# A decode step of gated attention and FFN: the block's barrier moved from behind the stores to behind wo's first piece

## Chip, cores and metric

The kernel runs on one core of a Trainium2 chip. The metric is the device time of one execution in microseconds (us); the times given are medians of several runs. The trace comes from one further execution under the hardware profiler, and its own time is given beside its span, which runs from the program's first to its last instruction.

The engines are named as in the profile: PE (TensorE; PEld are its weight loads), DVE (VectorE), ACT (ScalarE), POOL (GpSimd) and SP (SyncE). A "q" behind an engine's name marks what its sequencer does: it issues DMAs, drains, branches and handles semaphores.

## The reference

One token x (512 values, bf16) goes through two branches, which a gate mixes:

```python
g = sigmoid((x * gate_w).sum())
a = attention(x @ wq, k_cache, v_cache) @ wo      # 32 heads, 8 kv heads, 32768 keys of 128
b = (silu(x @ w_gate) * (x @ w_up)) @ w_down      # 512 -> 1792 -> 512
out = g * a + (1 - g) * b                         # 512 values
```

Each of 8 groups (g) has its own K and V cache of 32768 x 128 values, which 4 query heads share. The two caches are 64 MB each in bf16, the weights some 13 MB; all of it is read once.

## The kernel before

It is written engine by engine, in one block: each engine has a program of its own (`@block.sync`, `@block.tensor`, and so on), and they meet through semaphores alone. At the block's end every engine drains its work, adds to a semaphore, and waits for a release that POOL gives when all have come. This is the block's barrier; a like one stands ahead of the block.

**Loads.** SP issues all loads in one queue, in the order in which they are needed: wq, x and gate_w, w_gate and w_up, then for each group two K and two V blocks of 4 MB each into a ring of pages, each issue waiting until its page is free. Behind the last V block come w_down (`wd`) and wo. wo has 4 MB and is loaded in five pieces, of 8, 10, 8, 4 and 2 of its 32 row blocks (`WO_CUTS`, line 59), each with its own semaphore `sem_wo[k]`. They go into the page that held wq, so they are issued as soon as the V load ahead of them is.

**Attention.** In a loop over groups, PE transposes the K rows as pairs (line 372) and DVE copies them to SBUF (637); PE makes the scores (384); DVE takes maxima (642, 644), POOL reduces them over the partitions (254), ACT takes the exponentials with their sums (540); PE sums the V rows weighted with them into `ps_o` (429), ACT copies that (552), and PE adds up its parts (410).

**The end.** It is part of PE's last trip through the loop, `emit_end` (463). PE sums the exponentials over the partitions (465) and DVE makes the scaled heads `O2` out of them (660 to 676). The output row is summed in two places. `emit_wide` (439) multiplies a 128 x 512 block of wd or wo by one column and adds to `ps_w` (in the profile under `pst`, line 441), in four strips. `emit_rows` (450) multiplies a block in four quarters, each into rows of its own of `ps_c` (line 453). The order is: 8 blocks of wd; the transposition matmul of O2 (479); wo's piece 0 (8 blocks); the other 6 blocks of wd; piece 1 (10 blocks). Then DVE copies `ps_w` to `part` (680), PE adds the four strips of `part` into `ps_c` (the join, line 502), and pieces 2, 3 and 4 follow with `emit_rows`. DVE casts the sum into `res_row` (682), and SP and ACT each store a half of it (`store`, line 203). POOL waits for both stores (257), and then the block's barrier ends the program.

PE's wait for a piece of wo stands in line 487, its waits for the copy and for `O2z` in 500 and 501. `sem_pe_w` and `sem_dve_w` carry the join, `sem_pe_sum` and `sem_dve_row` the end.

Of the kernel before, what the change touches and what calls it, by code (L numbers as in the profile page):

```python
# [13 lines left out]
def bass_gated_mix__gqa_block_cached__swiglu_ffn__decode_kernel(  # L14
# [24 lines left out]
    FC = F // 128  # L39
# [15 lines left out]
    WOJ = H * DH // 128  # L55
# [3 lines left out]
    WO_CUTS = [0, 8, 18, 26, 30, 32]  # L59
    KW = 1  # L60
    WD_CUT = 8
    WIDE = WO_CUTS[KW + 1]
    OC = NOUT // 128

    RQ = 4
    NSTRIP = 4
    RPS = 2
    SW = 32
# [8 lines left out]
    with ExitStack() as es:  # L77
# [6 lines left out]
        sem_wo = [S_(f"s_wo{i}") for i in range(len(WO_CUTS) - 1)]  # L84
# [6 lines left out]
        sem_out = S_("s_out")  # L91
# [10 lines left out]
        sem_pe_sum = S_("s_pe_sum")  # L102
# [11 lines left out]
        sem_dve_oz = S_("s_dve_oz")  # L114
        sem_dve_row = S_("s_dve_row")
        sem_psw = S_("s_psw")
        sem_pe_w = S_("s_pe_w")
        sem_dve_w = S_("s_dve_w")
# [34 lines left out]
        tT = T("tT", [128, FC], BF16)  # L153
        wd = T("wd", [128, FC, NOUT], BF16)
# [9 lines left out]
        sel5 = T("sel5", [128, SW + 15], FP32)  # L164
# [7 lines left out]
        O2 = T("O2", [128, WOJ], BF16)  # L172
        O2z = T("O2z", [128, WOJ - WIDE, SW], BF16)
        part = T("part", [128, NOUT], FP32)
        res_row = T("res_row", [128, 128], BF16)
# [17 lines left out]
        ps_c = pst[1][:, 0:512]  # L193
        ps_w = pst[0][:, 512:1024]
# [5 lines left out]
        wgu = page[:, PG_F, 0 : 2 * KC * F].rearrange("p (w c f) -> p w c f", w=2, c=KC)  # L200
        wo_v = page[:, PG_X, 0 : WOJ * NOUT].rearrange("p (j n) -> p j n", j=WOJ)

        def store(eng, k):
            n = RPS * 128
            eng.dma_start(
                out[0, 0, n * k : n * (k + 1)].rearrange("(c n) -> c n", c=RPS),
                res_row[64 * k + SW - 1 : 64 * k + SW + 1, :],
            ).then_inc(sem_out, 16)

        with nc.Block("main") as block:  # L210
            @block.gpsimd
            def _(pool):
                pool.memset(ones_bf[:, :], 1.0).then_inc(sem_const, 1)
                pool.memset(ones_f[:, :], 1.0).then_inc(sem_const, 1)
                npool = [0]

                def chain(ins):
                    ins.then_inc(sem_pool, 1)
                    npool[0] += 1
                    pool.wait_ge(sem_pool, npool[0])  # L220

                pool.load_library(library_config.all_libraries[1])

                def ones_where(t, base, pattern):
                    return pool.affine_select(
                        out=t,
                        in_=t,
                        compare_op=ALU.not_equal,
                        fill=1.0,
                        base=base,  # L230
                        pattern=pattern,
                        channel_multiplier=1,
                    )

                pool.memset(ident[:, :], 0.0)
                pool.memset(ident_f[:, :], 0.0)
                pool.memset(perm[:, :, :], 0.0)
                pool.memset(sel5[:, :], 0.0)
                chain(pool.memset(pmat[:, :], 0.0))
                ones_where(ident[:, :], 0, [[-1, 128]]).then_inc(sem_ident, 1)  # L240
                ones_where(ident_f[:, :], 0, [[-1, 128]]).then_inc(sem_ident, 1)
                for e in range(2):
                    ones_where(perm[:, e, :], -e, [[0, 2], [-2, 64]]).then_inc(sem_ident, 1)
                ones_where(pmat[:, :], 0, [[-1, 32], [-32, 4]]).then_inc(sem_ident, 1)
                for c in range(NSTRIP):
                    chain(ones_where(sel4, -32 * c, [[-1, 16]]))
                pool.sem_inc(sem_ident, 1)
                pool.wait_ge(sem_dve_gpart, 1)
                pool.partition_all_reduce(gtot[:, :], gpart[:, :], 128, ReduceOp.add).then_inc(
                    sem_gtot, 1  # L250
                )
                for g in range(G):
                    pool.wait_ge(sem_pmax, STEP * (g + 1))
                    pool.partition_all_reduce(  # L254
                        gmax[:, g, :], pmax[:, g * STEP : g * STEP + HPG], 128, ReduceOp.max
                    ).then_inc(sem_gmax, 1)
                pool.wait_ge(sem_out, 32)

            @block.sync
            def _(sp):  # L260
# [47 lines left out]
                sp.wait_ge(sem_pe_q, 1)  # L308
                for k in range(len(sem_wo)):
                    load_wo(k)  # L310
                sp.wait_ge(sem_dve_row, 1)
                store(sp, 0)

            @block.tensor
            def _(pe):
                pe.wait_ge(sem_ld_x, 32)
                pe.wait_ge(sem_const, 1)
                for src, base in ((x_row, M_X0), (gw_row, M_X0 + KC)):
                    srcv = src[0:1, :].rearrange("o (p c) -> o c p", c=KC)
                    for c in range(KC):  # L320
# [4 lines left out]
                            start=True,  # L325
                            stop=True,
# [5 lines left out]
                for h in range(H):  # L332
                    for c in range(KC):
# [4 lines left out]
                            start=(c == 0),  # L338
# [97 lines left out]
                        )  # L436
                    ins.then_inc(sem_v_free, 1)

                def emit_wide(w, vec, j, first, last):
                    c = j % NSTRIP  # L440
                    return pe.matmul(  # L441
                        ps_w[32 * c : 32 * c + 1, :],
                        vec[:, j : j + 1],
                        w[:, j, :],
                        start=first,
                        stop=last,
                        skip_group_check=True,
                    )

                def emit_rows(lhs, rhs, first, last):  # L450
                    for oc in range(OC):
                        e = oc % RPS
                        ins = pe.matmul(  # L453
                            ps_c[32 * oc : 32 * oc + (1 if e else SW), 0:128],
                            lhs(e),
                            rhs[:, oc * 128 : (oc + 1) * 128],
                            start=first,
                            stop=last,
                            skip_group_check=True,
                        )  # L460
                    return ins

                def emit_end():
                    pe.wait_ge(sem_dve_esum2, 1)
                    pe.matmul(  # L465
                        ps_e[:, 0:H],
                        ones_f[:, :],
                        esum2[:, :, :].rearrange("p g h -> p (g h)"),
                        start=True,
                        stop=True,  # L470
                    ).then_inc(sem_pe_S, 1)
                    emit_reduce((G + 1) * STEP)
                    pe.wait_ge(sem_dve_tT, 1)
                    pe.wait_ge(sem_ld_wd, 16)
                    pe.wait_ge(sem_psw, 1)
                    for j in range(WD_CUT):
                        emit_wide(wd, tT, j, j < NSTRIP, False)
                    pe.wait_ge(sem_dve_oT2, 1)
                    pe.matmul(
                        ps_m[:, M_O0 : M_O0 + WOJ], pmat[:, :], O2a[:, :], start=True, stop=True  # L480
                    ).then_inc(sem_pe_O2, 1)
                    pe.wait_ge(sem_dve_O2, 1)
                    for k, s in enumerate(sem_wo):
                        if k == 1:
                            for j in range(WD_CUT, FC):
                                emit_wide(wd, tT, j, False, False)
                        pe.wait_ge(s, 16)
                        for j in range(WO_CUTS[k], WO_CUTS[k + 1]):
                            if j < WIDE:
                                ins = emit_wide(wo_v, O2, j, False, j >= WIDE - NSTRIP)  # L490
                            else:
                                ins = emit_rows(
                                    lambda e: O2[:, j : j + 1] if e else O2z[:, j - WIDE, :],
                                    wo_v[:, j, :],
                                    False,
                                    j == WOJ - 1,
                                )
                        if k == KW:
                            ins.then_inc(sem_pe_w, 1)
                            pe.wait_ge(sem_dve_w, 1)  # L500
                            pe.wait_ge(sem_dve_oz, 1)
                            emit_rows(lambda e: sel5[:, SW - 1 : SW] if e else sel5[:, 0:SW], part, True, False)
                    ins.then_inc(sem_pe_sum, 1)

                with pe.Fori(0, (G + 1) * STEP, STEP) as i:
                    for b in range(NB):
# [13 lines left out]
            def _(act):  # L520
# [37 lines left out]
                    if g:  # L558
                        emit_acc(g - 1)
                emit_acc(G - 1)  # L560
                act.wait_ge(sem_dve_row, 1)
                store(act, 1)

            @block.vector
            def _(dve):
# [110 lines left out]
                dve.tensor_copy(  # L676
                    O2z[:, :, SW - 1], ps_m[:, M_O0 + WIDE : M_O0 + WOJ]
                ).then_inc(sem_dve_oz, 1)
                dve.wait_ge(sem_pe_w, 1)
                dve.tensor_copy(part[:, :], ps_w[:, :]).then_inc(sem_dve_w, 1)  # L680
                dve.wait_ge(sem_pe_sum, 1)
                dve.tensor_copy(res_row[:, :], ps_c[:, 0:128]).then_inc(sem_dve_row, 1)


# [26 lines left out]
```

## Time and profile before

| what | us |
|---|---|
| median of 3 runs | 352.69 (352.42 to 352.89) |
| profiled execution, its own time | 352.48 |
| its span | 350.7 |
| PE busy | 269.5 (77% of the span) |
| DVE busy | 176.9 (50%) |
| ACT busy | 32.1 (9%) |
| DMA: 148.25 MB | 423 GB/s |

Busy time is the time in which an engine works on at least one instruction; on PE, matmuls overlap and their ends are modelled, so a busy PE isn't PE at its best. The page cuts the span into 40 slices and gives each a digit, its busy share in tenths. The chain that ended last is followed back from the last instruction to what released it. A group of instructions is named by line, engine, operation and its output and inputs.

The span doesn't hold the whole of the measured time: 352.48 - 350.7 = 1.78 us lie ahead of the first or behind the last of the program's own instructions.

### The profile page before, as it was taken

The numbers are of one execution on the slowest core, as the hardware profiler recorded it, in microseconds if no ns is written. First come the engines' busy times: TensorE is split into PE (matmuls) and PEld (weight loads), VectorE is DVE, ScalarE is ACT, GpSimd is POOL, SyncE is SP. The second block draws the span as 40 slices with busy tenths as digits, with TensorE's granted clock in tenths as the row PEclk, the third lists the DMA queues.
The fourth block names the chain that finished last, engine by engine and source line by source line (L and its number), as shares of the span: only waits on it lengthen the run. The fifth ranks groups of instructions, "written<-read, shape, count | busy, mean of one in ns | idle before, by whom it ended". The sixth has DMA issues, their size and how long they took to land.

```text
span 350.7 us, 8919 instructions
## 1 busy us (share of the span) xinstructions
PE 269.5 (77%) x4005; PEld 232.4 (66%) x4005; DVE 176.9 (50%) x193; ACT 32.1 (9%) x148; POOL 6.9 (2%) x29
## 2 busy tenths in 40 slices
PE   0446987898999959796797949696898959795584
PEld 0446987887796939495785839394876849493232
DVE  0010878474783928365472828175653819184011
ACT  1000000500030040002100040003000040004000
POOL 4000000000000000000000000000000000000000
PEclk9999989696998999889696989679886969679565
DMA  8999999999999999999999999999999999999995
GB/s 329 418 448 417 437 430 439 418 430 426 445 434 422 430 431 441 430 430 422 445 434 426 430 426 445 430 426 426 441 437 426 426 430 445 430 426 426 422 419 218
DMA packets 5925, 148.25 MB, mean 423 GB/s; under 512 B 666, under 2 KB 668, under 8 KB 924
## 3 DMA queue, kind: packets, MB, share of 16 engines
q1 hardware_dynamic: 5912, 148.12, 98.5%
q8 instruction: 7, 0.11, 0.1%
q14 instruction: 2, 0.02, 0.0%
q10 hardware_dynamic: 4, 0.00, 0.0%
HBM read 148.11 MB, written 0.00 MB: 422 GB/s over the span
## 4 chain that ended last, share of the span: by engine, by line
DMA 64%; PE 31%; DVE 2%; SPq 1%; issue 1%
DMA page<-in_A_k_cache_dram 53%; PE pst L372 23%; DMA page<-in_A_wo_dram 11%; PE ps_sc L384 5%; DVE ktT L637 2%; PE ps_o L429 1%; PE pst L453 1%; PE pst L441 0%; PE ps_m L410 0%; SPq L283 0%; SPq L262 0%; DVE part L680 0%; SPq L305 0%; SPq L300 0%; SPq L279 0%
## 5 line engine op out<-in xcount | busy, mean ns | idle before, releaser
L637 DVE COPY ktT<-pst 128x2048 bf16<-128x2048 bf16 x128 | 156.1, 1224 | 106.5 <-PE pst L372 99.4
L372 PE MATMUL pst<-ident_f,page 128*128 128x128 f32 x1024 | 160.2, 315 | 40.2 <-DMA page<-in_A_k_cache_dram 38.8
L372 PEld LDWEIGHTS pst<-ident_f,page 128*128 128x128 f32 x1024 | 137.2, 164 | 50.6 <-DMA page<-in_A_k_cache_dram 46.7
L384 PEld LDWEIGHTS ps_sc<-qcur,ktT 128*128 128x128 bf16 x2048 | 67.0, 97 | 11.4 <-DVE ktT L637 10.0
L384 PE MATMUL ps_sc<-qcur,ktT 128*128 128x8 bf16 x2048 | 67.9, 166 | 8.6 <-DVE ktT L637 8.6
L429 PE MATMUL ps_o<-page,ET 128*16 128x512 bf16 x512 | 42.1, 487 | 4.6 <-DMA page<-in_A_v_cache_dram 4.6
L429 PEld LDWEIGHTS ps_o<-page,ET 128*16 128x16 bf16 x512 | 13.3, 104 | 23.2 <-issue 10.7
L531 ACT ACTIVATE nbias<-gmax 128x4 f32<-128x4 f32 x8 | 1.6, 205 | 263.6 <-POOL gmax L254 263.6
L540 ACT ACTIVATE ET<-ps_sc,nbias 128x128 bf16<-128x128 f32 x64 | 23.9, 554 | 0.6
L540 ACT ACTIVATION_READ_ACCUMULATOR ET<-ps_sc,nbias 128x1 f32 x64 | 18.2, 284 | 0.0
L642 DVE TENSOR_REDUCE pmaxf<-ps_sc 128x4 f32<-128x512 f32 x16 | 11.1, 691 | 11.5 <-PE ps_sc L384 11.5
L410 PE MATMUL ps_m<-sel,acc 128*128 128x4 f32 x72 | 10.8, 273 | 3.7 <-ACT acc L552 3.7
L410 PEld LDWEIGHTS ps_m<-sel,acc 128*128 128x128 f32 x72 | 10.1, 217 | 4.3 <-ACT acc L552 4.3
L358 PE MATMUL ps_m<-xT,page 128*128 128x1 bf16 x112 | 6.9, 198 | 4.8 <-DMA page<-in_B_w_up_dram 4.8
L321 PE MATMUL ps_m<-ones_bf,x_row 1*128 1x1 bf16 x4 | 0.3, 174 | 13.1 <-DMA gw_row<-in_gate_w_dram 13.1
L358 PEld LDWEIGHTS ps_m<-xT,page 128*128 128x128 bf16 x112 | 6.8, 162 | 4.9 <-DMA page<-in_B_w_up_dram 4.9
L254 POOL PARTITION_ALL_REDUCE gmax<-pmax x8 | 3.0, 373 | 302.7 <-DVE pmax L644 302.7
L321 PEld LDWEIGHTS ps_m<-ones_bf,x_row 1*128 1x128 bf16 x4 | 0.2, 116 | 13.1 <-DMA gw_row<-in_gate_w_dram 13.1
L552 ACT ACTIVATE acc<-ps_o 128x512 f32<-128x512 f32 x8 | 5.2, 653 | 13.6 <-PE ps_o L429 13.6
L660 DVE RECIPROCAL rS<-pst 128x32 f32<-128x32 f32 x1 | 0.4, 359 | 12.1 <-PE pst L465 12.1
L577 DVE CAST xT<-ps_m 128x4 bf16<-128x4 f32 x1 | 0.2, 163 | 12.1 <-PE ps_m L321 12.1
L616 DVE TENSOR_TENSOR t<-sg,ps_m 128x14 f32<-128x14 f32 x1 | 0.2, 170 | 10.7 <-ACT sg L525 10.7
(65 smaller groups left out, 38.4 us busy)
## 6 DMA issues: line engine op xcount, KB each, us to landing
page<-in_A_k_cache_dram SPq DMA_DIRECT2D x16, 4096.0 KB, 27.2
page<-in_A_v_cache_dram SPq DMA_DIRECT2D x16, 4096.0 KB, 31.1
page<-in_A_wq_dram SPq DMA_DIRECT2D x1, 4096.0 KB, 12.2
page<-in_A_wo_dram SPq DMA_DIRECT2D x2, 1024.0 KB, 38.8
page<-in_B_w_gate_dram SPq DMA_DIRECT2D x1, 1792.0 KB, 15.4
page<-in_B_w_up_dram SPq DMA_DIRECT2D x1, 1792.0 KB, 20.6
wd<-in_B_w_down_dram SPq DMA_DIRECT2D x1, 1792.0 KB, 34.5
page<-in_A_wo_dram SPq DMA_DIRECT2D x1, 1280.0 KB, 39.1
```

Of the source, the lines that this page charges most:

```text
L254: pool.partition_all_reduce(gmax[:, g, :], pmax[:, g * STEP : g * STEP + HPG], 128, ReduceOp.max).then_inc(sem_gmax, 1)
L358: ins = pe.matmul(ps_m[:, base + j : base + j + 1], wgu[:, w, c, :].rearrange("d (p j) -> d j p", j=FC)[:, j, :], xT[:, c : c + 1], start= ...
L372: ins = pe.transpose(pst[u % NST][:, k * 128 : (k + 1) * 128], kv[:, n * 128 : (n + 1) * 128], ident_f[:, :],)
L384: ins = pe.matmul(ps_sc[b][:, col : col + 2 * HPG], kt[:, k, e, :], qcur[:, e, :], start=(e == 0), stop=(e == 1),)
L410: ins = pe.matmul(ps_m[:, M_P0 : M_P0 + HPG], acc[:, q, :], sel4[:, q * HPG : (q + 1) * HPG], start=(q == 0), stop=(q == RQ - 1),)
L429: ins = pe.matmul(ps_o[32 * c : 32 * c + RQ * HPG, :], ET[:, n : n + RQ, :].rearrange("p n h -> p (n h)"), view[:, k * RQ : (k + 1) * RQ, ...
L453: ins = pe.matmul(ps_c[32 * oc : 32 * oc + (1 if e else SW), 0:128], lhs(e), rhs[:, oc * 128 : (oc + 1) * 128], start=first, stop=last, sk ...
L531: act.activation(nbias[:, g, :], gmax[:, g, :], ACT.Copy, scale=-SCALE).then_inc(sem_nbias, 1)
L540: act.activation(ET[:, b * R : (b + 1) * R, h], sc[:, h, :], ACT.Exp, bias=nbias[:, g, h : h + 1], scale=SCALE, accum_out=esum[:, g, b, h ...
L552: act.activation(acc[:, :, :].rearrange("p q d -> p (q d)"), ps_o[:, :], ACT.Copy).then_inc(sem_acc, STEP)
L637: dve.tensor_copy(ktT[:, u % NKT, :], pst[u % NST][:, :].bitcast(BF16)).then_inc(sem_cp, 1)
L642: dve.tensor_reduce(pmaxf[:, b, :], sc, AX.X, ALU.max).then_inc(sem_pmax, 4)
```

## The change

The block ends earlier. PE's part of the block ends behind wo's piece 0 and the other 6 blocks of wd; DVE's behind `O2z`; ACT's behind its last copy of `ps_o`; SP's behind the issue of wo's five pieces; POOL's behind its last reduction. Behind the block's barrier stand, outside any block, on PE the pieces 1 to 4 of wo with the join, on DVE the copy of `ps_w` and the cast, on SP and ACT the two stores. POOL no longer waits for the stores: SP does, as the last instruction of the program, and nothing comes behind it. No other barrier is added.

`emit_wide`, `emit_rows` and the loop over a piece (now `emit_wo`) move ahead of the block, with the engine as an argument, and are otherwise as they were. The diff, cut to its core:

```diff
+        def emit_wo(pe, k):
+            pe.wait_ge(sem_wo[k], 16)
+            for j in range(WO_CUTS[k], WO_CUTS[k + 1]):
...
@@ in @block.gpsimd
-                pool.wait_ge(sem_out, 32)
@@ in @block.sync
-                sp.wait_ge(sem_dve_row, 1)
-                store(sp, 0)
@@ in emit_end, @block.tensor
-                    for k, s in enumerate(sem_wo):
-                        if k == 1:
-                            for j in range(WD_CUT, FC):
-                                emit_wide(wd, tT, j, False, False)
-                        pe.wait_ge(s, 16)
...
+                    for k in range(KW):
+                        emit_wo(pe, k)
+                    for j in range(WD_CUT, FC):
+                        emit_wide(pe, wd, tT, j, False, False)
@@ in @block.scalar
-                act.wait_ge(sem_dve_row, 1)
-                store(act, 1)
@@ in @block.vector
-                dve.wait_ge(sem_pe_w, 1)
-                dve.tensor_copy(part[:, :], ps_w[:, :]).then_inc(sem_dve_w, 1)
-                dve.wait_ge(sem_pe_sum, 1)
-                dve.tensor_copy(res_row[:, :], ps_c[:, 0:128]).then_inc(sem_dve_row, 1)
+
+        pe, dve = nc.tensor, nc.vector
+        for k in range(KW, len(sem_wo)):
+            ins = emit_wo(pe, k)
+            if k == KW:
+                ins.then_inc(sem_pe_w, 1)
+                pe.wait_ge(sem_dve_w, 1)
+                pe.wait_ge(sem_dve_oz, 1)
+                emit_rows(
+                    pe, lambda e: sel5[:, SW - 1 : SW] if e else sel5[:, 0:SW], part, True, False
+                )
+        ins.then_inc(sem_pe_sum, 1)
+        dve.wait_ge(sem_pe_w, 1)
+        dve.tensor_copy(part[:, :], ps_w[:, :]).then_inc(sem_dve_w, 1)
+        dve.wait_ge(sem_pe_sum, 1)
+        dve.tensor_copy(res_row[:, :], ps_c[:, 0:128]).then_inc(sem_dve_row, 1)
+        for k, eng in enumerate((nc.sync, nc.scalar)):
+            eng.wait_ge(sem_dve_row, 1)
+            store(eng, k)
+        nc.sync.wait_ge(sem_out, 32)
```

More of the change, by code (lines that the diff above doesn't have):

```diff
@@ L201, in bass_gated_mix__gqa_block_cached__swiglu_ffn__decode_kernel, with emit_wide, emit_rows @@
         wo_v = page[:, PG_X, 0 : WOJ * NOUT].rearrange("p (j n) -> p j n", j=WOJ)
+        def emit_wide(pe, w, vec, j, first, last):
+            c = j % NSTRIP
+            return pe.matmul(
+                ps_w[32 * c : 32 * c + 1, :],
+                vec[:, j : j + 1],
+                w[:, j, :],
+                start=first,
+                stop=last,
+                skip_group_check=True,
+            )
+        def emit_rows(pe, lhs, rhs, first, last):
+            for oc in range(OC):
+                e = oc % RPS
+                ins = pe.matmul(
+                    ps_c[32 * oc : 32 * oc + (1 if e else SW), 0:128],
+                    lhs(e),
+                    rhs[:, oc * 128 : (oc + 1) * 128],
+                    start=first,
+                    stop=last,
+                    skip_group_check=True,
+                )
+            return ins
+        def emit_wo(pe, k):
+            pe.wait_ge(sem_wo[k], 16)
+            for j in range(WO_CUTS[k], WO_CUTS[k + 1]):
+                if j < WIDE:
+                    ins = emit_wide(pe, wo_v, O2, j, False, j >= WIDE - NSTRIP)
+                else:
+                    ins = emit_rows(
+                        pe,
+                        lambda e: O2[:, j : j + 1] if e else O2z[:, j - WIDE, :],
+                        wo_v[:, j, :],
+                        False,
+                        j == WOJ - 1,
+                    )
+            return ins
         def store(eng, k):
@@ L437, in emit_v @@
                     ins.then_inc(sem_v_free, 1)
[L439 to L461, printed above, removed]
                 def emit_end():
@@ L476, in emit_end @@
                     for j in range(WD_CUT):
-                        emit_wide(wd, tT, j, j < NSTRIP, False)
+                        emit_wide(pe, wd, tT, j, j < NSTRIP, False)
                     pe.wait_ge(sem_dve_oT2, 1)
@@ L482, in emit_end @@
                     pe.wait_ge(sem_dve_O2, 1)
-                    for k, s in enumerate(sem_wo):
-                        if k == 1:
-                            for j in range(WD_CUT, FC):
-                                emit_wide(wd, tT, j, False, False)
-                        pe.wait_ge(s, 16)
[L488 to L503, printed above, removed]
+                    for k in range(KW):
+                        emit_wo(pe, k)
+                    for j in range(WD_CUT, FC):
+                        emit_wide(pe, wd, tT, j, False, False)
                 with pe.Fori(0, (G + 1) * STEP, STEP) as i:
@@ L678, in _ @@
                 ).then_inc(sem_dve_oz, 1)
-                dve.wait_ge(sem_pe_w, 1)
-                dve.tensor_copy(part[:, :], ps_w[:, :]).then_inc(sem_dve_w, 1)
-                dve.wait_ge(sem_pe_sum, 1)
-                dve.tensor_copy(res_row[:, :], ps_c[:, 0:128]).then_inc(sem_dve_row, 1)
+        pe, dve = nc.tensor, nc.vector
[7 more added lines that the diff above has]
+                    pe, lambda e: sel5[:, SW - 1 : SW] if e else sel5[:, 0:SW], part, True, False
+                )
+        ins.then_inc(sem_pe_sum, 1)
[7 more added lines that the diff above has]
+        nc.sync.wait_ge(sem_out, 32)
 _INS = ['A_x', 'A_k_cache', 'A_v_cache', 'A_wq', 'A_wo', 'B_x', 'B_w_gate', 'B_w_up', 'B_w_down', 'gate_w']
```

## The prediction

> **What bounds the kernel now.** I read the page first: the span, the busy row of the DMA engines and the chain that ended last.
>
> ```profile
> span 350.7 us, 8919 instructions
> ...
> DMA  8999999999999999999999999999999999999995
> ...
> DMA 64%; PE 31%; DVE 2%; SPq 1%; issue 1%
> ```
>
> The DMA engines are busy in every slice but the first and the last, so the weights and caches stream without a break and the kernel is bound by that stream up to its end. Nothing in the change touches the stream or its order. What it can move lies behind it, so the next view is the chain in order of time, from the last transfers on.
>
> ```profile
> 343.75 0.04 issue
> 343.79 1.46 PE pst L441 x9
> ...
> 346.02 1.50 PE pst L453 x38
> ...
> 347.55 0.61 PE pst L453 x14
> 348.16 0.03 issue
> 348.19 0.43 PE pst L453 x4
> ...
> 348.65 0.29 DVE res_row L682
> ```
>
> The columns are start, duration and what ran. The stream hands over to TensorE when wo's second piece lands, at 343.75. From there TensorE and VectorE run nearly without a gap to the cast that ends at 348.65 + 0.29 = 348.94: the pauses named issue are 0.02 to 0.04 us. So whatever starts TensorE's work on the second piece later makes the whole rest later by as much, but for a few hundredths. What happens ahead of 343.75 on the other engines is free.
>
> The timeline ends with the two store issues, and a look at line 210 (the block) lists what comes with and behind them. Its rows give duration in ns (min/median/max) and first and last start in us.
>
> ```profile
> 348.97 0.27 SPq L205 DMA_DIRECT2D out_dram<-res_row  x1
> 348.98 0.60 ACTq L205 DMA_DIRECT2D out_dram<-res_row  x1
> ```
>
> ```profile
> L210 POOLq EVENT_SEMAPHORE  x2: 17/17/17, 350.5 to 350.6; - x2
> L210 PEldq DRAIN  x1: 124/124/124, 348.6 to 348.6; - x1
> L210 DVEq DRAIN  x1: 330/330/330, 348.7 to 348.7; - x1
> L210 SPq DRAIN  x1: 206/206/206, 349.3 to 349.3; - x1
> L210 ACTq DRAIN  x1: 143/143/143, 349.6 to 349.6; - x1
> L210 POOLq COMPARE_BRANCH  x1: 33/33/33, 350.3 to 350.3; - x1
> L210 POOLq DRAIN  x1: 41/41/41, 350.4 to 350.4; - x1
> L210 SPq EVENT_SEMAPHORE  x1: 17/17/17, 350.6 to 350.6; - x1
> ...
> L210 PEldq EVENT_SEMAPHORE  x1: 51/51/51, 350.6 to 350.6; - x1
> ```
>
> Four engines arrive at the block's barrier between 348.6 and 349.8 (ACT: 349.6 + 0.14). POOL's branch carries the wait for both stores, and starts at 350.3: that is when the stores have landed. Then come POOL's drain at 350.4, its two semaphore steps at 350.5 and 350.6, and the release of the four others at 350.6. The span ends at 350.7. So **0.4 us of barrier stand behind the last store**, and they are on the path, since nothing else is left.
>
> The profiled execution took 352.48 us against its span of 350.7: 1.78 us lie outside the program's own instructions. It is 0.21 below the median of the runs shown (352.69); I sum against the profiled execution and subtract the result from the median.
>
> **The change, part by part.**
>
> 1. *The barrier behind the stores goes.* The order of instructions in the changed program has nothing behind SP's wait for both stores, and POOL, PE, DVE and ACT have no wait for them at all. The wait is over at the same 350.3, and its instruction is of the kind that takes SP 17 ns. The span then ends at 350.3 instead of 350.7: **-0.4 us**. Both ends are read to a tenth, so the term is 0.3 to 0.5.
>
> 2. *The barrier now stands between wo's first and second piece.* For it all five engines must have finished what is left in the block.
>
> ```profile
> 341.23 0.84 PE L441 MATMUL pst<-wd,tT 128*1 128x512 bf16 x6
> ...
> 340.49 0.21 DVE L676 CAST O2z<-ps_m 128x14 bf16<-128x14 f32 x1
> ...
> 337.62 0.60 ACT L552 ACTIVATE acc<-ps_o 128x512 f32<-128x512 f32 x1 [13.56 <-PE ps_o L429]
> ...
> 304.17 2.33 SPq L300 DMA_DIRECT2D page<-in_A_wo_dram  x5
> ```
>
> PE is last, at 341.23 + 0.84 = 342.07 (the six matmuls of w_down's rest); DVE is done at 340.70, ACT at 338.22, SP at 306.50, and POOL's last reduction, on whose maximum ACT's last exponentials wait, lies earlier than ACT's end. How long the barrier takes from there has two rows: the one at the end, from POOL's drain at 350.4 to the last release, 0.3 us (with PE's own drain of 0.12 us ahead: 0.4), and the one with which the program starts, in the next fence.
>
> ```profile
> L696 POOLq EVENT_SEMAPHORE  x2: 17/17/17, 0.5 to 0.6; - x2
> L696 SPq DRAIN  x1: 7/7/7, 0.0 to 0.0; - x1
> L696 PEldq DRAIN  x1: 8/8/8, 0.3 to 0.3; - x1
> L696 PEldq EVENT_SEMAPHORE  x1: 51/51/51, 0.7 to 0.7; - x1
> ```
>
> That one takes 0.7 us from the first engine's arrival. So PE is released at 342.5 to 342.8, and the second piece lands at 343.75: 1.0 us of cover or more. I take **0**. Behind PE's added wait stand the second piece's ten matmuls, and for them DVE's copy into part, the join, the rest of wo and the stores; none of them is ready before 343.75 in any case. DVE waits in the barrier with the copy behind it, which needs those matmuls; ACT and SP wait with their stores behind it, which need the cast. If the cover were gone, each us of delay would be a us of time, by the chain above.
>
> 3. *SP's stream passes the barrier.* All of SP's loads are issued by 306.50, ahead of it in program order; only the store stands behind. SP's arrival doesn't wait for what it has in flight: in the rows above SP drains at 349.3 + 0.21 = 349.5, when its store is still 0.8 us from having landed (350.3). So wo's pieces still under way, the last of which PE takes up only at 348.19, don't hold the barrier. 0.
>
> 4. *Moved code and the same instructions.* The matmuls, the two DVE copies, and both stores are the same ones in the same order on the same engines and queues, and no instruction is added but the wait, which moves from POOL to SP. 0, with the 0.1 us of difference that a wait on another engine may make.
>
> 5. *What lies outside the span.* 1.78 us follow or precede the program, and no view shows its inside. Before, all five engines come into it together, at 350.6 to 350.7, so the slowest of them sets how soon the common end work starts. After, the four others come early (the last of them is ACT, whose issue ends at 348.98 + 0.60 = 349.58, 0.7 us ahead of 350.3), and SP alone comes late. The nearest rows for how far apart engines get between two such points are those at the program's start: SP stands at its first instruction at 0.0 and PE at 0.3. So this term is between 0 (SP is itself the slowest) and -0.3, or as much as -0.5 if the spread at the end is larger than at the start. I take **-0.2**, near the middle.
>
> [...]
>
> **Sum:** -0.4 + 0 + 0 + 0 - 0.2 = -0.6 us. 352.48 - 0.6 = 351.88 for the profiled execution; from the median, 352.69 - 0.6 = **352.1 us**, that is -0.17%. A measurement of this kernel can tell about 0.2%, 0.7 us, from no change. So the likeliest result is a real gain that stays just within that bound.
>
> **The rivals.**
>
> *A: the forecast.* A gain of 0.3 to 0.7, 352.0 to 352.4. For it speaks that the 0.4 us at the end are plain in the rows.
>
> *B: more comes outside the span.* If the engines' ways into the end work lie 0.3 to 0.5 apart and SP's is the shortest, the gain is 0.7 to 0.9 and the time 351.8 to 352.0. For it: SP is the first at the start (0.0), PE the last (0.3). Against it: nothing shows that order at the end.
>
> *C: the end isn't set by the span's end.* If some other engine's end work is the longer one, or the program gets its barrier anyway, the span may shorten but the time stays: 352.5 to 352.7. For it: 1.78 us of which no view tells who sets them. [...]
>
> *D: the release comes behind wo's second piece (slower).* The place is PE's wait in the moved barrier; it decides from a release at 343.75 on, and with 0.6 us of gain it is slower than before from 344.4 on, by over 0.2% from 345.1 on. It would come about if SP's drain waited for its five loads: the last of them is used at 348.19, so PE would start at about 348.6 instead of 343.79, 4.8 us late, and the time would be 352.1 + 4.8 = 356.9. Against it stands SP's drain of part 3.
>
> *E: a jump that isn't in the instruction buffer.* After the block PE goes on in another part of its program; if that had to be fetched, PE would stand still behind the barrier. One fetch is in the transfers of the last 3 us.
>
> ```profile
> q8 instruction: 1, 0.02, 2.0%
> ```
>
> 2.0% of 16 engines over 3 us is 0.96 us for one fetch. With the store's delay for a small transfer, from its issue's end at 349.24 (or 349.58) to 350.3, as the other bound, the stall is 1.0 to 2.0 us behind a release at 342.5 to 342.8: PE starts between 343.5 (nothing lost) and 344.8 (1.0 late). One miss gives 352.1 to 353.1, two in a row 353.1 to 354.1. Against it: PE left the same loop for the same kind of place before, and its drain stood at 348.6, right behind its last matmul (348.19 + 0.43 = 348.62).
>
> [...]
>
> **How the numbers follow.** A 0.47, B 0.31, C 0.14, D 0.03, E 0.05. The predicted time is A's, 352.1. Faster by over 0.2% (below 352.0): B and a little of A's edge, 0.33. Within 0.2%: the rest of A, C, and E with one miss, 0.61. Slower: D and E with two, 0.06. The range: B's lower end of 351.8, less 0.3 for the runs' own spread (352.42 to 352.89), 351.5; above, C's 352.7 and a little of that spread, 352.8. D and E's worse half lie outside it.
>
> **What would show it.** Right: the span 0.4 shorter (about 350.3); SP's wait for the stores its last row; the barrier's drains and semaphores at 342 to 343, PE's at the latest; TensorE's second piece still starting 0.04 us behind its landing; the cast still ending about 5.2 us behind that landing; the time outside the span at 1.78 or less. Wrong: a gap between wo's second landing and its first matmul (D, E), barrier rows behind the stores (C), the time outside the span grown by what the span lost (C), or shrunk by more than 0.3 (B).

## The result and the profile after

| | before | changed |
|---|---|---|
| median of 16 runs, us | 352.58 (352.38 to 352.89) | 351.58 (351.38 to 352.98) |
| ratio, with 95% interval | | 0.998 (0.9971 to 0.9988) |
| profiled execution, us | 352.48 | 351.52 |
| its span, us | 350.7 | 350.2 |
| outside the span, us | 1.78 | 1.32 |

The change gains: 0.2% by the ratio, 0.7 us, between 0.4 and 1.0 us by its interval. The medians lie 1.0 us apart. The two differ because the runs of the changed kernel are uneven: ten of the 16 lie between 351.38 and 351.77, six between 352.08 and 352.98. So there are two things to explain, the gain, and why a third of the runs lose 0.3 us of it or more.

The page of the changed kernel, its span, its fetches of code and its chain:

```profile
span 350.2 us, 8919 instructions
...
DMA  8999999999999999999999999999999999999995
...
q8 instruction: 6, 0.10, 0.1%
...
DMA 64%; PE 32%; DVE 2%; SPq 1%; issue 1%
```

The stream is as it was. The moved barrier is line 249 now; its rows, with duration in ns (min/median/max) and first and last start in us:

```profile
L249 POOLq EVENT_SEMAPHORE  x2: 17/17/17, 342.3 to 342.3; - x2
L249 SPq DRAIN  x1: 122/122/122, 306.5 to 306.5; - x1
L249 POOLq DRAIN  x1: 487/487/487, 319.7 to 319.7; - x1
L249 ACTq DRAIN  x1: 607/607/607, 337.6 to 337.6; - x1
L249 DVEq DRAIN  x1: 353/353/353, 340.3 to 340.3; - x1
L249 PEldq DRAIN  x1: 1162/1162/1162, 341.1 to 341.1; - x1
...
L249 PEldq EVENT_SEMAPHORE  x1: 51/51/51, 342.4 to 342.4; - x1
```

PE comes last: its drain starts at 341.1 and ends at 342.3, when the six matmuls of w_down are through. PE is released at 342.4. SP came at 306.5 and its drain took 0.12 us, with all of wo still under way. The chain behind it, in order of time:

```profile
343.70 0.04 issue
343.74 1.46 PE pst L205 x10
...
345.23 0.70 DVE part L685
...
348.12 0.43 PE pst L217 x4
...
348.58 0.29 DVE res_row L687
```

The second piece starts 0.04 us behind its landing at 343.70, as before, and from there to the cast's start it is 4.84 us (348.58 - 343.74), before 4.86. The barrier in the middle is free: 1.3 us lie between the release and the landing. The last row of the program is now SP's wait (line 691):

```profile
L691 SPq EVENT_SEMAPHORE  x1: 17/17/17, 350.2 to 350.2; - x1
```

The span ends with it.

### The profile page after: what moved, and what is told of

Read it like the earlier page. It is cut to its first block, busy times and chain, and to the rows that moved or that the text cites. A ratio compares the mean times of both kernels' runs of the same rounds, so it can differ in the third digit from the quotient of the medians.

```text
span 350.2 us, 8919 instructions
## 1 busy us (share of the span) xinstructions
PE 269.0 (77%) x4005; PEld 230.9 (66%) x4005; DVE 176.8 (50%) x193; ACT 32.3 (9%) x148; POOL 6.9 (2%) x29
## 4 chain that ended last, share of the span: by engine, by line
DMA 64%; PE 32%; DVE 2%; SPq 1%; issue 1%
DMA page<-in_A_k_cache_dram 53%; PE pst L408 24%; DMA page<-in_A_wo_dram 11%; PE ps_sc L420 5%; DVE ktT L630 1%; PE ps_o L465 1%; PE pst L217 1%; PE pst L205 0%; PE ps_m L446 0%; SPq L321 0%; SPq L300 0%; DVE part L685 0%; SPq L343 0%; SPq L338 0%; SPq L317 0%
## 5 line engine op out<-in xcount | busy, mean ns | idle before, releaser
L465 PE MATMUL ps_o<-page,ET 128*16 128x512 bf16 x512 | 43.2, 497 | 4.6 <-DMA page<-in_A_v_cache_dram 4.6
```

What stands on the lines that cost most here:

```text
L465: ins = pe.matmul(ps_o[32 * c : 32 * c + RQ * HPG, :], ET[:, n : n + RQ, :].rearrange("p n h -> p (n h)"), view[:, k * RQ : (k + 1) * RQ, ...
```

## The experiments

Each was run beside the kernel before on the same chip; "span" and "outside" are medians over its runs, outside being a run's time less its span. Three chips were used, on which the kernel before hardly differs. The changed kernel again, POOL last, the second barrier and the block that ends behind piece 1 ran on one (before: span 350.8, outside 1.81, 33 runs). PE last, the block that ends behind all of wo, and the changed kernel with 80 and with 40 more matmuls ran on another (350.7 and 1.83, 29 runs), and the other three on a third (350.7 and 1.82, 25 runs).

### The changed kernel again, and four places for the last wait

**The changed kernel again.**

> The changed kernel once more, as the partner of the three others on the same chip. Theory L (the last engine to end its program sets what follows the span; SP is quick to get there): span 350.1 to 350.3, most runs 351.4 to 351.6, so 1.3 us outside the span, and again about a third of the runs 0.5 to 1.4 us longer, all of it outside the span. Rival S (the longer third is chance of one chip or one session): all runs 351.4 to 351.8.

Measured: 351.66 us (351.39 to 352.52, 11 runs), ratio 0.9976 (0.9967 to 0.9985); span 350.3, outside 1.35. The 0.9 us of gain are 0.5 in the span and 0.46 outside it. Two of eleven runs have 1.61 and 2.02 outside, all others 1.29 to 1.44: S falls. L's third of longer runs, by 0.5 to 1.4, was too much: two of eleven, by 0.26 and 0.67.

**POOL waits for the stores.**

```diff
-        nc.sync.wait_ge(sem_out, 32)
+        nc.gpsimd.wait_ge(sem_out, 32)
```

> The changed kernel with POOL in the place of SP as the engine that waits for the stores; still no barrier behind. Theory L: the span stays at 350.2, but the time outside it grows from 1.3 toward the 1.8 us that it had before, since in the kernel before too POOL was the engine that let the barrier go: 351.8 to 352.0. Rival N (it doesn't matter who waits; the gain outside the span came from the other four engines being early): 351.5, as the partner.

Measured: 352.29 us (352.04 to 353.0, 11 runs), ratio 0.9994 (0.9985 to 1.0003); span 350.4, outside 1.89. One wait on another engine, and of the 0.46 us outside nothing is left. The program itself ends at the same point, as the row of line 691 shows:

```profile
L691 POOLq EVENT_SEMAPHORE  x1: 17/17/17, 350.4 to 350.4; - x1
```

So the time outside depends on which engine comes out of the program last: 1.89 us with POOL, 1.35 with SP. N falls and L holds, though its total of 351.8 to 352.0 was 0.3 too low: both the span and the time outside came out longer than it said.

**A second barrier behind SP's wait.**

```diff
         nc.sync.wait_ge(sem_out, 32)
+        nc.all_engine_barrier()
```

> The changed kernel with a second barrier of all engines behind SP's wait: the moved barrier costs what it costs, and the old end is back. Theory L: 0.4 us more span (350.6) and 1.8 us outside it, 352.4 to 352.6, the time of the kernel before; the barrier in the middle costs 0. Rival M (moving the barrier between wo's pieces gained or cost something by itself): different from the kernel before by that much, in the span.

Measured: 352.49 us (352.33 to 353.15, 11 runs), ratio 1.0 (0.9991 to 1.0009); span 350.7, outside 1.9. That is the kernel before, with one more barrier in its middle: M falls, the move by itself is free. The rows of the added barrier (line 692):

```profile
L692 POOLq EVENT_SEMAPHORE  x2: 17/17/17, 350.5 to 350.6; - x2
...
L692 SPq DRAIN  x1: 7/7/7, 350.5 to 350.5; - x1
...
L692 PEldq EVENT_SEMAPHORE  x1: 51/51/51, 350.7 to 350.7; - x1
```

From SP's arrival at 350.5 to PE's release at 350.7 the four others do nothing but wait for one that has to go through the same end.

**PE waits for the stores.**

```diff
-        nc.sync.wait_ge(sem_out, 32)
+        nc.tensor.wait_ge(sem_out, 32)
```

> The changed kernel with PE as the engine that waits for the stores, no barrier behind. Theory L (the waiting engine's own way into what follows the span sets the time outside; each engine has its own): the span 350.3 to 350.4, outside between SP's 1.35 and POOL's 1.89, so 1.4 to 1.6, and 351.7 to 352.0 in all. Rival Q (POOL alone is slow, the others alike): 1.35 outside, 351.65, as with SP.

Measured: 352.17 us (351.87 to 353.03, 11 runs), ratio 0.9991 (0.9982 to 1.0); span 350.3, outside 1.77, with 1.57 the least (SP's least is 1.29 and POOL's 1.82). Q falls. The least value fits L, the median is above what L said, and the values are spread from 1.57 to 2.43. This ran on another chip than SP and POOL last; on this one the versions with SP last (below) have 1.26 to 1.45 outside in 27 of 29 runs.

**SP waits, but inside the block of the kernel before.**

```diff
-                pool.wait_ge(sem_out, 32)
...
                 store(sp, 0)
+                sp.wait_ge(sem_out, 32)
```

> The kernel before with one edit: inside the block SP waits for the stores in the place of POOL; the block and its barrier stay behind the stores. Theory L (with a barrier at the end POOL releases the others and is the last to go on, whoever waited): within 0.15 us of the kernel before, span 350.7 to 350.8, outside 1.8. Rival W (the gain outside the span came from POOL being rid of the wait itself): outside falls toward 1.35, 352.1.

Measured: 352.63 us (352.3 to 353.71, 12 runs), ratio 1.0009 (0.9999 to 1.0018); span 350.7, outside 1.8, as the kernel before beside it (350.7 and 1.82). W falls: with a barrier behind it, it doesn't matter which of the two waits. Four of the twelve runs are long ones, with 2.69 to 2.98 outside.

### What an uncovered barrier costs

**The block ends behind piece 1.**

```diff
                     for j in range(WD_CUT, FC):
                         emit_wide(pe, wd, tT, j, False, False)
+                    emit_wo(pe, KW).then_inc(sem_pe_w, 1)
...
```

> The changed kernel with the block ending one piece of wo later, behind piece 1, so that its barrier stands between piece 1's matmuls and DVE's copy of their sum, on the chain. Theory C (the barrier is free only for the cover ahead of piece 1's landing; uncovered it costs its length one to one): the copy starts 0.3 to 0.45 us later behind the last matmul of piece 1 and the span is 0.25 to 0.45 longer than the partner's, 350.5 to 350.6. Rival F (slack further down, at the landing of the last piece, takes it up): the span within 0.1 of the partner's.

Measured: 351.75 us (351.45 to 352.01, 11 runs), ratio 0.9974 (0.9965 to 0.9983); span 350.4, outside 1.34. C falls, and F holds: the barrier did delay the copy, as C said, but not the end. The timeline of DVE, and the weight loads that waited for transfers, in this kernel:

```profile
345.71 0.69 DVE L686 COPY part<-pst 128x512 f32<-128x512 f32 x1 [4.87 <-PEq L249]
348.77 0.29 DVE L688 CAST res_row<-pst 128x128 bf16<-128x128 f32 x1 [2.37 <-PE pst L217]
```

```profile
343.94 0.10 PEld L205 LDWEIGHTS pst<-page,O 128*1 128x1 bf16 x8 [2.48 <-DMA page<-in_A_wo_dram]
...
348.32 0.10 PEld L217 LDWEIGHTS pst<-page,O2z 128*32 128x32 bf16 x1 [0.20 <-DMA page<-in_A_wo_dram]
```

And the same two in the changed kernel beside it:

```profile
345.39 0.69 DVE L685 COPY part<-pst 128x512 f32<-128x512 f32 x1 [4.59 <-PE pst L205]
348.76 0.29 DVE L687 CAST res_row<-pst 128x128 bf16<-128x128 f32 x1 [2.68 <-PE pst L217]
```

```profile
343.91 0.10 PEld L205 LDWEIGHTS pst<-page,O 128*1 128x1 bf16 x8 [2.47 <-DMA page<-in_A_wo_dram]
...
347.65 0.10 PEld L217 LDWEIGHTS pst<-page,O2z 128*32 128x32 bf16 x1 [0.28 <-DMA page<-in_A_wo_dram]
348.31 0.10 PEld L217 LDWEIGHTS pst<-page,O2z 128*32 128x32 bf16 x1 [0.31 <-DMA page<-in_A_wo_dram]
```

In brackets stands how long the engine sat idle and what ended it. From the first load of piece 1 to the copy it is 1.48 us in the changed kernel (345.39 - 343.91) and 1.77 here (345.71 - 343.94): the barrier costs 0.29. But the changed kernel's weight loads wait 0.28 us for piece 3 and 0.31 for piece 4. With the delay, the wait for piece 3 is gone and that for piece 4 is 0.20; the last piece starts 348.32 against 348.31. The landings gave the delay back.

**The block ends behind all of wo.** All matmuls and the copy stand in the block, only the cast and the stores behind it.

```diff
                     for j in range(WD_CUT, FC):
                         emit_wide(pe, wd, tT, j, False, False)
+                    for k in range(KW, len(sem_wo)):
+                        ins = emit_wo(pe, k)
...
+                    ins.then_inc(sem_pe_sum, 1)
...
```

> The changed kernel with the block ending behind the last piece of wo: all of PE's work and the copy are in the block, the cast and the stores behind its barrier. The barrier then stands behind the last transfer, where no landing takes up a delay. Theory F' (a barrier costs its length, 0.3 us, only where no later landing gives it back; behind piece 1 the two waits of 0.3 us for the pieces 3 and 4 gave it back): the cast starts 0.3 to 0.4 us later behind the last matmul, the span is 350.6 to 350.7, outside 1.35, 351.95 to 352.1. Rival Z (a barrier among engines that have all come costs nothing anywhere): span 350.3, 351.65.

Measured: 351.86 us (351.74 to 352.97, 11 runs), ratio 0.9984 (0.9975 to 0.9993); span 350.6, outside 1.3. Here no landing follows:

```profile
348.18 0.10 PEld L217 LDWEIGHTS pst<-page,O2z 128*32 128x32 bf16 x1 [0.30 <-DMA page<-in_A_wo_dram]
```

```profile
348.92 0.29 DVE L687 CAST res_row<-pst 128x128 bf16<-128x128 f32 x1 [2.95 <-PEq L249]
```

From the last piece to the cast it is 0.74 us (348.92 - 348.18) against 0.45 above (348.76 - 348.31). The cast waited for PE's side of the barrier (PEq L249). F' holds with 0.29 us, and the span is 0.3 longer than the changed kernel's 350.3. Z falls. The total that F' said was 0.1 to 0.2 too high; the time outside came to 1.3, not 1.35.

### Why single runs take longer

Up to here, SP alone waits at the end in 49 runs (16 and 11 of the changed kernel, 11 with the block ending behind piece 1, 11 with it ending behind all of wo). Twelve of them have 1.5 us or more outside the span, up to 2.78, and the others 1.26 to 1.45. The execution that was profiled with POOL last happens to be a long one of its kind: 353.0 us with a span of 350.4, 2.6 outside, where that kernel's median is 1.89. Its transfers in the window from 348 to 354 us, 0.15 us to a digit:

```profile
DMA  0000000000000000000000000000400000000000
...
q8 instruction: 1, 0.02, 1.0%
```

The two stores are too small to show. The one busy slice, at 352.2, is a fetch of code, 1.0% of 16 engines over 6 us, or 0.96 us long; it starts when the program has been over for 1.8 us. It ends at 352.2 + 0.96 = 353.16 or later. Counted from the span's start, this execution was over at 353.0 at the latest, so it can't have waited for the fetch to end, if the two clocks agree to 0.1 us. On the page of the changed kernel q8 counts six fetches within the span, on that of before seven:

```profile
q8 instruction: 7, 0.11, 0.1%
```

That is 0.11 / 7 MB, about 16 KB, each. So the author's theory was that PE's last instructions lie near the border between two such fetches, and that some executions end up waiting for the second; more instructions near the start would move that border away from the end.

**80 more matmuls on PE near the start** (160 instructions, in PE's pause ahead of w_up; the two permutation matmuls of q are repeated, the result is the same).

```diff
-                for e in range(2):
+                for e in [0, 1] * 41:
                     ins = pe.matmul(
                         ps_o[:, e * H : (e + 1) * H],
```

> The changed kernel with 80 more matmuls on PE (160 instructions) near the start, the two permutation matmuls of q repeated 40 times while PE waits for w_up; the result is the same. It moves PE's last instructions to another place in the pages of its code. Theory P (the runs that take 0.3 to 1.5 us longer outside the span wait at the very end for one more page of PE's code, of which the trace with POOL last shows a late fetch): the seventh fetch comes well ahead of the end, and all runs have 1.27 to 1.40 outside, 351.4 to 351.8 in all. Rival G (the longer runs come from something else that follows the span): a quarter to a third of them have 1.5 or more, as before.

Measured: 351.62 us (351.47 to 352.88, 9 runs), ratio 0.997 (0.9957 to 0.9983); outside 1.27 to 1.36 in all nine. G falls for the time outside. But two runs have longer spans, 351.0 and 351.6 against 350.2 to 350.4; the profiled execution is one, with its second piece starting at 345.08:

```profile
345.04 0.04 issue
345.08 1.46 PE pst L205 x6
```

There the transfers came 1.3 us late, and nothing of it lies at the end. A fetch of this kernel, by the author's count the seventh, comes between 68 and 71 us, in the loop; of that window:

```profile
q8 instruction: 1, 0.02, 2.1%
```

**40 more matmuls** (`[0, 1] * 21`).

> The same with 40 more matmuls (80 instructions). Theory P: as with 160 if 80 are enough to bring the seventh fetch ahead of the last microseconds, all runs 1.27 to 1.40 outside; the trace shows the fetch before 348. Rival G: longer runs as before, whatever the fetch does.

Measured: 351.59 us (351.41 to 351.75, 9 runs), ratio 0.9973 (0.9963 to 0.9983); outside 1.28 to 1.45, spans 350.1 to 350.4. What P said of the times holds: no run is longer. The transfers in the window from 346 to 349 us hold a fetch:

```profile
q8 instruction: 1, 0.02, 2.3%
```

**The kernel before with the same 40 matmuls.**

> The kernel before with the 40 more matmuls on PE near the start. Theory P (the late page of PE's code is what makes single runs of either kernel longer): its median stays at 352.5 to 352.6, and none of its runs has more than 1.95 outside the span, where the kernel before has up to 3.3. Rival G: single runs up to 2.4 and more stay.

Measured: 352.58 us (352.39 to 354.41, 12 runs), ratio 1.0009 (0.9998 to 1.0019); outside 1.74 to 1.84 in all twelve, where the kernel before beside it has up to 2.34. What P said holds again for the time outside. But five of the twelve spans are 351.1 to 352.6, the others 350.6 to 350.8. Here too a fetch comes in the loop; of the window from 67 to 70 us:

```profile
q8 instruction: 1, 0.02, 2.1%
```

**The changed kernel with 40 more matmuls, again.**

> The changed kernel with 40 more matmuls once more, beside the kernel before with the same 40: all runs 1.27 to 1.45 outside and 351.4 to 351.8; the difference to the padded kernel before is what the change does when no page of code comes late, 0.45 in the span and 0.45 outside, 0.9 in all.

Measured: 351.71 us (351.45 to 351.80, 7 runs), ratio 0.9972 (0.9961 to 0.9983); outside 1.30 to 1.35, spans 350.1 to 350.5. Against the padded kernel before the medians lie 0.87 apart: 0.4 in the span and 0.47 outside.

All in all, none of the 25 runs of the changed kernel with added matmuls has more than 1.45 outside, against twelve of 49 with 1.5 or more without them (on the one chip that had both, none of 18 against two of 11). The twelve runs of the kernel before with added matmuls have 1.84 at most, where five of the 25 beside them without have 1.99 to 2.34. So with the added instructions the long ends did not come.

That a late fetch makes them is not shown. The changed kernel beside the others has a fetch ahead of the program's end, at 349.5 in the window from 348 to 354 us, and its profiled execution is a short one (351.71 us, 1.31 outside):

```profile
DMA  0000000000500000000000000000000000000000
...
q8 instruction: 1, 0.02, 1.3%
```

The kernel with the block ending behind all of wo is alike: a fetch at 349.95, and 1.26 outside. With the block ending behind piece 1, the trace has six fetches and none from 348 to 354 us, yet its profiled execution is one of the twelve long ones (352.01 - 350.4 = 1.61):

```profile
q8 instruction: 6, 0.10, 0.1%
```

So of the four profiled executions with SP last and no added matmuls, the two with a fetch near the end are short (1.31 and 1.26 outside), and the one long one (1.61) has none.

The changed kernel with 40 more matmuls is the best version tried: its median is that of the changed kernel, but its 16 runs stay between 351.41 and 351.80.

## Why the prediction was right

The direction is right and the time is in the range, but only just: 351.58 lies 0.08 above its lower end and below the likeliest case, A (352.0 to 352.4). The gain by the ratio, 0.7 us, lies where A and B meet, and by the sign that the prediction gave for B, a time outside the span shrunk by more than 0.3, it is B that came, which had 0.31. Two terms were too small, the span by 0.1 and the time outside by 0.26, and the median of three runs from which the sum went was 0.11 above that of the 16 (352.58). That the time is still in the range is owed to the 0.3 that the range adds below B for the spread of the runs, which has nothing to do with these terms; that part is luck.

1. *The barrier behind the stores.* -0.4 was said, 0.3 to 0.5; the span went from 350.7 to 350.2, and from 350.8 to 350.3 in the medians of many runs. Right, with 0.5 at the upper end of what was said. The second barrier gave it back (350.7).

2. *The moved barrier is free.* Right, in its reason too: PE was released at 342.4, just ahead of the 342.5 to 342.8 that was forecast, and 1.3 us ahead of the landing.

3. *SP's drain doesn't wait for transfers under way.* Right: 0.12 us at 306.5. D's route through it is excluded.

4. *Who waits makes 0.1 us of difference.* Wrong by itself: with POOL in SP's place it was 0.54 us outside the span (1.89 against 1.35). The step took the wait as an instruction of 17 ns and didn't ask what its engine has to do behind it.

5. *Outside the span.* -0.2 was taken, from the spread of the engines at the start (0.3); -0.46 came. The mechanism was the one named, that the last engine out sets the time outside (1.35 us with SP alone behind, 1.89 with POOL alone, 1.9 with all five behind a barrier), and the size was off: the nearest row was one of another place. What the runs showed is rival B's case, that SP's way is the shortest, at least of the three engines tried (ACT and DVE were not): 1.29 at the least with SP, 1.57 with PE, 1.82 with POOL, and 1.73 with a barrier behind all. The profiled execution gained 0.96 us, more than B's 0.7 to 0.9. The longer runs pull the mean of the 16 back to 351.87, and the gain by the ratio to 0.7.

6. *"The whole rest later by as much, but for a few hundredths."* Wrong, though nothing hung on it in the sum. The pauses named issue in the chain hid slack: the same trace has these two rows for the weight loads of the kernel before.

```profile
347.54 0.10 PEld L453 LDWEIGHTS pst<-page,O2z 128*32 128x32 bf16 x1 [0.29 <-DMA page<-in_A_wo_dram]
348.19 0.10 PEld L453 LDWEIGHTS pst<-page,O2z 128*32 128x32 bf16 x1 [0.30 <-DMA page<-in_A_wo_dram]
```

PE's matmuls overlap and their ends are modelled, so PE looked busy up to each landing, while its weight loads had stood still for 0.3 us. The block ended behind piece 1 put a delay of 0.29 there, and the end didn't move. D's price, which moved all the rest by 4.8 us, would have been lower by these two waits, 0.6 us.

7. *E, a jump to code that must be fetched.* No stall stood behind the moved barrier: the second piece started 0.04 us behind its landing. E's price for two misses doesn't follow from its price for one: 1.0 to 2.0 us each behind the release make 2.0 to 4.0, so PE would start between 344.5 and 346.8, and the time would be 352.8 to 355.1, not 353.1 to 354.1. What the prediction didn't look at is the end of PE's code: twelve of 49 runs lose 0.2 to 1.4 us outside the span, and none of the 25 with matmuls added on PE does. C falls: the 0.5 us by which the span became shorter came through to the time.

What stays open: what makes single runs long outside the span. With matmuls added on PE none of 25 runs was long there, against twelve of 49; that this hangs on the length of PE's code is the author's reading, that a late fetch of code is what such a run waits for is only a guess, and the traces speak in part against it. It is open too why the changed kernel with 80 more matmuls and the kernel before with 40 have single longer spans (351.0 and 351.6; 351.1 to 352.6). Why the median with PE last lies 0.2 above its least value was not tried with added matmuls.

## What to carry to other kernels

In these runs, a barrier behind the last store was pure time (0.4 to 0.5 us of span), one ahead of a landing that all the rest waits for was free (released 1.3 us before it), and where later landings left slack it was free even on the chain (0.29 us later at the copy, 0.01 at the last piece). What ends the program should be one wait, on the engine with the shortest way out, and that is found by trying the engines, since no view of the span shows it. Read slack from the waits of the weight loads, not from the pauses in the chain: on the kernel before the first show 0.29 and 0.30 us, the second 0.02 and 0.03.

## What was not expected of the hardware

- The time outside the span depends on the engine that ends last: 1.35 us with SP, 1.77 with PE (on another chip), 1.89 with POOL, with the same span of 350.3 to 350.4.
- A barrier of all five engines on the path cost 0.29 us, measured twice (behind piece 1 and ahead of the cast).
- With 40 to 80 more matmuls on PE, which cost the median nothing (351.59 to 351.71 us against 351.58 and 351.66), none of 25 runs of the changed kernel ended late outside the span; without them 12 of 49 did, by 0.2 to 1.4 us. The reason is open.
